# Two raw quads in the second MLP activation buffer, and a new order of operations searched with late transfers

## The chip, the cores and the metric

One core of a Trainium2 chip runs the whole program. The time is the device time of one execution in microseconds (us), given as the median of several executions.

PE is the matrix engine, PEld its weight loads, DVE the vector engine, ACT the scalar engine, POOL and SP two more engines that also issue transfers.

## The reference, cut to what matters

Random-feature attention on 8 batches of 8 heads, and then a mixer with a low-rank mix over the sequence and an MLP:

```python
proj = einsum('bhsd,md->bhsm', x, omega)             # for q and for k
phi  = concatenate([cos(proj), sin(proj)]) / sqrt(m)
kv   = einsum('bhsm,bhsd->bhmd', k_p, v);  z = sum(k_p)
num  = einsum('bhsm,bhmd->bhsd', q_p, kv); den = q_p . z
x    = num / den                                     # (8, 576, 512) after joining the heads
u    = x + (low-rank mix over the sequence with U, V)
out  = u + relu(u @ w_ch1) @ w_ch2                   # w_ch1: 512 x 2048
```

## The kernel before

The whole program is one list of words, ORDER, read from left to right. Each word emits one operation on one engine. Every engine runs its operations in that order, so **a word's place in the list is its place in the queue of its engine**; semaphores do the rest. `@n` names the first of the eight banks of PSUM (the memory that matmuls write) for the result; a bank is free again once another engine has copied it out.

```python
def run(self, order):
    for word in order.split():
        ...
        _, emit, needs, takes, frees = self.ops[name]
        if takes:
            self.banks[name] = range(int(at), int(at) + takes)   # PSUM banks, asserted free
        emit()
        for n in frees: ...                                      # banks free again
```

A *quad* is four heads: a q half and a k half (288 KB each as stored) and a v of 576 KB. A quad feeds two *groups* of two heads, and four groups make a batch: quads 0 and 1 feed groups 0 to 3, which are batch 0, while quads 2 and 3 belong to batch 1. The words that the argument needs:

```text
ld/k/2 ld/q/2  load the k or q half of raw quad 2 (POOL's queue)     ldv/1  load v of quad 1 (SP's queue)
tpp/q/2 tp/q/2 transpose that half on PE, copy it out on DVE         wv/1   widen v of quad 1 (POOL)
ak/5 uk/5      k angles of group 5: matmul on PE, "angle operation" on DVE (aq, uq the same for q)
s/4 c/4        sine, cosine of group 4 (ACT); p/4 the quarter turn between them (POOL)
kv/2 kvb/2     kv product of group 2 (PE), its copy out (DVE)        num/1  numerator of group 1 (PE)
x/3            normalised x of group 3 (DVE): the FOURTH x, batch 0 is then complete
w1/0/0         first complete W1 step of batch 0 (w1p: parts of it, ahead)    d  warmer: a dummy matmul
```

The raw buffers, two for q and k, and the load rule:

```python
rawp = ctx.enter_context(tc.tile_pool(name="rawp", bufs=2))
hidp = ctx.enter_context(tc.tile_pool(name="hidp", bufs=2))      # MLP activations, two buffers
...
def load(name, n):
    if ("raw", n) not in held:
        held["raw", n] = rawp.tile([P, 2, 2, NS * D], BF16, name="raw")
    return held["raw", n][:, "kq".index(name), :, :]
...
need = [r for r in read_raw(name, n - NRAW)] if n >= NRAW else []     # NRAW = 2: wait for the place
add(("ld", name, n), POOL, lambda ...: nc.gpsimd.dma_start(load(name, n), quad(src, n)), needs=need)
...
held["v", n] = rawp.tile([P, 2, NS * D], F32, name="vraw", bufs=2)
(nc.sync if n else nc.gpsimd).dma_start(held["v", n], quad(v, n))     # v of quad 0 by POOL, the rest by SP
```

The ORDER of the opening, cut, with banks and warmers left out:

```text
... ld/k/0 ... ld/q/0 ... ld/k/1 ... ld/q/1 ... ldv/0 omb ... ukh/0/0 ld/k/2 tp/q/0/0 ...
sq/0 tpp/q/1 ck/0 ldv/1 pq/0 tp/k/1 aq/1 tp/q/1 ld/q/2 cq/0 uq/1 ... W1/0 ldv/2 kv/0/0 ld/k/3 uq/2 ...
kvb/0 tpp/k/2 uq/3 tpp/q/2 c/1 p/2 num/0 ... x/0 ak/4 ld/q/3 wv/1 ... num/1 ... x/1 num/2 ... x/2 ... num/3 ... x/3 ...
tpp/k/3 ... tp/k/3 ... ak/5 ... uk/5 ... w1/0/0
```

Of the kernel before, what the change touches and what calls it, by code (L numbers as in the profile page):

```python
# [20 lines left out]
R = 32  # L21
# [14 lines left out]
begin first/k/0 first/k/1 ident first/q/0 om ld/k/0 d/0@5 warm d/1@1 ld/q/0 d/2@0 ld/k/1 d/3@7 d/4@5 ld/q/1 d/5@0 cast/k/1 cast/k/0 d/6@2  # L36
ldv/0 omb d/7@0 tpp/k/0/0@3 tpp/k/0/1@4 omt@7 tp/k/0/0 cast/q/0 WT tpp/k/0/2@0 tp/k/0/1 akh/0/0@5 tp/k/0/2 tpp/q/0/0@7 tpp/q/0/1@1 ukh/0/0
ld/k/2 tp/q/0/0 akh/0/1@2 tp/q/0/1 ukh/0/1 aq/0@4 d/8@6 gate skh/0/0 uq/0 d/9@7 low ak/1@0 skh/0/1 at/0@3 d/10@6 ut/0 pk/0 tpp/k/1@6 uk/1
sq/0 tpp/q/1@4 ck/0 ldv/1 pq/0 tp/k/1 d/11@1 aq/1@1 tp/q/1 ld/q/2 cq/0 uq/1 ak/2@3 wv/0 aq/2@6 uk/2 d/12@1 s/1 W1/0 ldv/2 kv/0/0@0 ld/k/3
uq/2 ak/3@2 W1/1 kv/0/1 p/1 uk/3 s/2 aq/3@6 kvb/0 tpp/k/2@2 uq/3 tpp/q/2@4 c/1 p/2 num/0 tp/k/2 tp/q/2 d/13@2 sk/3 x/0 ak/4@5 ld/q/3 wv/1  # L40
kv/1/0@3 c/2 uk/4 kv/1/1 pk/3 aq/4@1 kvb/1 kv/2/0@6 uq/4 sq/3 kv/2/1 lowc num/1 ck/3 kvb/2 kv/3/0@1 x/1 num/2 pq/3 kv/3/1 ld/k/4 hu0/0@0
cq/3 kvb/3 ut0x/0@3 huc0/0 hu0/1@4 ld/q/4 x/2 ut0/0 s/4 ut0x/1@0 W1/2 d/14@5 num/3 huc0/1 W1/3 ute0/0 hu0/2@7 ut0x/2@4 ut0/1 huc0/2
w1p/0/0@3 x/3 p/4 ut0/2 ute0/1 tpp/k/3@5 ute0/2 w1p/2/0@0 w1p/2/1 tp/k/3 hu0/3@7 w1p/1/0@2 w1p/3/0@1 huc0/3 ak/5@4 wv/2 c/4 w1p/3/1 uk/5
w1p/1/1 w1p/1/2 ut0x/3@7 ut0/3 w1p/3/2 w1p/2/2 w1p/0/1 ute0h/3 w1p/0/2 tpp/q/3@4 ute0/3 tp/4 w1/0/0 tp/q/3 aq/5@6 r/0/0 w1/0/1 w1/0/2 uq/5
w1/0/3 r/0/1 hn/0/0@4 r/0/2 w1/0/4@3 u/0/0 r/0/3 ldv/3 w1/0/5@0 r/0/4 s/5 ak/6@4 aq/6@1 w1/0/6@3 uk/6 w1/0/7@7 r/0/5 p/5 uq/6 r/0/6
w1/0/8@5 r/0/7 ak/7@0 r/0/8 aq/7@3 s/6 kv/4/0@6 uk/7 W2/0 w1/0/9@5 W2/1 kv/4/1 uq/7 W2/2 w1/0/10@2 r/0/9 p/6 c/5 hn/0/1@0 kvb/4 w1/0/11@5
u/0/1 num/4 wv/3 r/0/10 w1/0/12@4 x/4 r/0/11 w1/0/13@0 W2/3 r/0/12 d/15@1 kv/5/0@5 r/0/13 kv/5/1 s/7 ak/8@0 kvb/5 aq/8@3 w2/0/0/0@7 uk/8
num/5 c/6 p/7 uq/8 w1/0/14@0 w2/0/0/1 x/5 r/0/14 kv/6/0@1 ld/k/5 kv/6/1 c/7 ak/9@3 ld/q/5 w1/0/15@0 uk/9 ld/k/6 hnt/0@6 w2/0/0/2 ld/q/6
r/0/15 kvb/6 ut/tail/0 s/8 kv/7/0@3 kv/7/1 aq/9@5 num/6 kvb/7 num/7 x/6 p/8 w2/0/0/3 x/7 w2/0/1/0@0 w2/0/1/1 o/0/0 c/8 uq/9 w2/0/1/2 tp/5
hu/1@1 w2/0/1/3 s/9 huc/1 w2/0/2/0@7 o/0/1 hn/1/0@5 ldv/4 w2/0/2/1 p/9 st/0/0 u/1/0 hn/1/1@0 w2/0/2/2 u/1/1 w2/0/2/3 c/9 tu/1 w2/0/3/0@0  # L50
o/0/2 ak/10@2 ak/11@5 uk/10 w2/0/3/1 wv/4 tp/6 w2/0/3/2 uk/11 aq/10@3 w2/0/3/3 uq/10 kv/8/0@6 ldv/5 kv/8/1 kv/9/0@1 st/0/1 s/10 kvb/8
aq/11@4 kv/9/1 num/8 kvb/9 st/0/2 uq/11 w1/1/0@3 ldv/6 p/10 num/9 x/8 r/1/0 w1/1/1@4 s/11 o/0/3 w1/1/2@5 x/9 ld/k/7 w1/1/3@6 r/1/1 wv/5
w1/1/4@7 r/1/2 r/1/3 hnt/1@2 p/11 w1/1/5@0 r/1/4 ut/tail/1 c/10 ak/12@4 w1/1/6@1 uk/12 ld/q/7 w1/1/7@2 r/1/5 ld/k/8 r/1/6 ak/13@5 ld/q/8
r/1/7 kv/10/0@3 uk/13 aq/12@0 c/11 kv/10/1 w1/1/8@2 uq/12 w1/1/9@7 r/1/8 aq/13@5 kvb/10 tp/7 kv/11/0@0 r/1/9 uq/13 kv/11/1 s/12 num/10
w1/1/10@2 kvb/11 x/10 num/11 s/13 p/12 w1/1/11@5 x/11 tp/8 w1/1/12@3 w1/1/13@6 r/1/10 wv/6 r/1/11 hu/2@1 r/1/12 w1/1/14@0 r/1/13 huc/2
ld/k/9 c/12 w1/1/15@2 ld/q/9 hn/2/0@6 p/13 w2/1/0/0@3 u/2/0 r/1/14 hn/2/1@4 r/1/15 w2/1/0/1 u/2/1 c/13 ak/14@0 aq/14@6 w2/1/0/2 tu/2 uk/14
w2/1/0/3 uq/14 w2/1/1/0@0 o/1/0 kv/12/0@1 ldv/7 s/14 kv/12/1 ldv/8 kv/13/0@6 kvb/12 ak/15@3 st/0/3 kv/13/1 num/12 kvb/13 uk/15 tp/9 p/14
num/13 w2/1/1/1 x/12 w2/1/1/2 c/14 w2/1/1/3 x/13 wv/7 aq/15@1 ak/16@3 o/1/1 w1/2/0@6 uq/15 ld/k/10 w1/2/1@7 r/2/0 uk/16 ak/17@0 r/2/1
w1/2/2@6 s/15 uk/17 w1/2/3@5 w1/2/4@3 r/2/2 p/15 w1/2/5@2 r/2/3 r/2/4 hnt/2@0 w1/2/6@5 r/2/5 ut/tail/2 ld/q/10 aq/16@3 r/2/6 aq/17@6
kv/14/0@1 wv/8 c/15 kv/14/1 w1/2/7@5 kvb/14 uq/16 ld/k/11 num/14 w2/1/2/0@0 uq/17 s/16 w1/2/8@3 x/14 w2/1/2/1 tp/10 r/2/7 p/16 w1/2/9@4  # L60
r/2/8 kv/15/0@1 r/2/9 ak/18@5 st/1/0 kv/15/1 uk/18 aq/18@3 c/16 w2/1/2/2 ldv/9 w2/1/2/3 ldv/10 kvb/15 st/1/1 num/15 s/17 w1/2/10@7 x/15
w2/1/3/0@5 uq/18 r/2/10 w1/2/11@1 o/1/2 kv/16/0@6 r/2/11 ak/19@2 kv/16/1 s/18 st/1/2 wv/9 uk/19 aq/19@0 w2/1/3/1 ldv/11 w2/1/3/2 uq/19
wv/10 w1/2/12@4 kvb/16 ld/q/11 hu/3@2 r/2/12 ld/k/12 num/16 huc/3 w2/1/3/3 p/17 x/16 w1/2/13@1 hn/3/0@2 r/2/13 p/18 w2/2/0/0@7 u/3/0 c/17
w1/2/14@6 w1/2/15@0 r/2/14 hnt/3@1 hn/3/1@2 r/2/15 w2/2/0/1 s/19 u/3/1 w2/2/0/2 o/1/3 w2/2/0/3 ut/tail/3 c/18 st/1/3 p/19 w2/2/1/0@5 o/2/0
ak/20@0 st/2/0 kv/17/0@6 uk/20 w2/2/1/1 ld/q/12 c/19 tu/3 aq/20@3 kv/17/1 uq/20 ak/21@0 w2/2/1/2 kvb/17 w2/2/1/3 uk/21 tp/11 num/17
w2/2/2/0@4 x/17 s/20 w2/2/2/1 tp/12 o/2/1 kv/18/0@0 kv/18/1 aq/21@6 p/20 kv/19/0@2 kvb/18 kv/19/1 num/18 kvb/19 st/2/1 uq/21 w2/2/2/2
w2/2/2/3 x/18 s/21 num/19 ld/k/13 w1/3/0@0 x/19 w1/3/1@1 p/21 r/3/0 o/2/2 w1/3/2@7 r/3/1 ak/22@3 r/3/2 aq/22@1 ld/q/13 w1/3/3@0 uk/22 c/20
ld/k/14 w2/2/3/0@7 uq/22 w2/2/3/1 r/3/3 c/21 kv/20/0@5 ak/23@0 aq/23@3 kv/20/1 uk/23 w2/2/3/2 tp/13 s/22 w2/2/3/3 kvb/20 w1/3/4@0 o/2/3
uq/23 num/20 ldv/12 p/22 r/3/4 st/2/2 w1/3/5@7 hu/4@1 r/3/5 st/2/3 w1/3/6@3 huc/4 s/23 x/20 w1/3/7@2 w1/3/8@0 r/3/6 p/23 hnt/4@6 r/3/7
w1/3/9@5 ut/tail/4 r/3/8 w1/3/10@3 r/3/9 w1/3/11@0 wv/11 r/3/10 c/22 hn/4/0@6 ld/q/14 hn/4/1@2 u/4/0 w1/3/12@1 ld/k/15 ld/q/15 w1/3/13@4  # L70
u/4/1 r/3/11 wv/12 r/3/12 w1/3/14@7 r/3/13 tu/4 w1/3/15@6 r/3/14 ak/24@3 r/3/15 ak/25@0 uk/24 c/23 w2/3/0/0@7 tp/14 w2/3/0/1 uk/25
w2/3/0/2 kv/21/0@5 kv/21/1 aq/24@0 ak/26@2 kvb/21 w2/3/0/3 uq/24 num/21 o/3/0 w2/3/1/0@0 x/21 st/3/0 w2/3/1/1 uk/26 w2/3/1/2 w1/4/0@1
w1/4/1@5 r/4/0 aq/25@6 r/4/1 kv/22/0@1 uq/25 kv/23/0@3 s/24 kv/22/1 kv/23/1 w1/4/2@5 kvb/22 kvb/23 num/22 p/24 num/23 x/22 s/25 w2/3/1/3
x/23 w1/4/3@6 r/4/2 w1/4/4@7 p/25 o/3/1 r/4/3 hu/5@4 c/24 st/3/1 w2/3/2/0@2 huc/5 w2/3/2/1 r/4/4 aq/26@0 kv/24/0@3 kv/24/1 ak/27@5 kvb/24
w2/3/2/2 uq/26 w2/3/2/3 uk/27 w1/4/5@0 w1/4/6@1 o/3/2 r/4/5 num/24 r/4/6 w1/4/7@0 c/25 x/24 hn/5/0@1 hn/5/1@5 u/5/0 w1/4/8@4 r/4/7
w1/4/9@7 u/5/1 r/4/8 w2/3/3/0@0 r/4/9 tu/5 s/26 w2/3/3/1 aq/27@1 kv/25/0@3 uq/27 kv/25/1 ak/28@5 p/26 w2/3/3/2 st/3/2 kvb/25 s/27 uk/28
w1/4/10@2 ldv/13 w1/4/11@1 ldv/14 r/4/10 w1/4/12@7 p/27 r/4/11 num/25 r/4/12 w2/3/3/3 x/25 w1/4/13@2 o/3/3 w1/4/14@4 r/4/13 wv/13 c/26
w1/4/15@3 w2/4/0/0@7 ldv/15 st/3/3 w2/4/0/1 r/4/14 r/4/15 aq/28@5 tp/15 kv/26/0@0 uq/28 ak/29@2 kv/26/1 w2/4/0/2 uk/29 s/28 w2/4/0/3
w2/4/1/0@6 o/4/0 c/27 kvb/26 w1/5/0@2 p/28 st/4/0 w2/4/1/1 w1/5/1@7 r/5/0 c/28 hnt/5@3 w2/4/1/2 ut/tail/5 w2/4/1/3 r/5/1 w2/4/2/0@3 o/4/1
w1/5/2@2 num/26 r/5/2 w1/5/3@7 x/26 w2/4/2/1 r/5/3 w2/4/2/2 kv/27/0@0 ak/30@4 kv/27/1 uk/30 w2/4/2/3 w1/5/4@2 o/4/2 w1/5/5@5 kvb/27 r/5/4  # L80
w1/5/6@4 r/5/5 num/27 r/5/6 aq/29@2 x/27 ak/31@4 w2/4/3/0@7 uq/29 w2/4/3/1 w1/5/7@1 uk/31 w1/5/8@2 r/5/7 w1/5/9@5 r/5/8 s/29 w1/5/10@6
w1/5/11@1 w2/4/3/2 r/5/9 p/29 r/5/10 hu/6@0 r/5/11 w2/4/3/3 w1/5/12@2 o/4/3 wv/14 huc/6 w1/5/13@6 r/5/12 c/29 hn/6/0@0 hn/6/1@4 u/6/0
w1/5/14@7 w2/5/0/0@2 u/6/1 r/5/13 r/5/14 w1/5/15@0 tu/6 w2/5/0/1 r/5/15 kv/28/0@6 aq/30@4 aq/31@0 kv/28/1 w2/5/0/2 kvb/28 st/4/1 uq/30
w2/5/0/3 st/4/2 uq/31 w2/5/1/0@3 s/30 w2/5/1/1 st/4/3 w2/5/1/2 p/30 w2/5/1/3 num/28 w2/5/2/0@0 x/28 c/30 w2/5/2/1 o/5/0 w1/6/0@7 o/5/1
st/5/0 s/31 w2/5/2/2 st/5/1 w1/6/1@2 w1/6/2@5 r/6/0 p/31 r/6/1 w1/6/3@1 w1/6/4@2 wv/15 c/31 w2/5/2/3 w1/6/5@4 o/5/2 w1/6/6@3 st/5/2 r/6/2
# [57 lines left out]
def kernel(  # L143
# [125 lines left out]
    def load(name, n):  # L269
        if ("raw", n) not in held:  # L270
            held["raw", n] = rawp.tile([P, 2, 2, NS * D], BF16, name="raw")
        return held["raw", n][:, "kq".index(name), :, :]
# [427 lines left out]
```

## Time and profile before

| | kernel before |
|---|---|
| timed median | 358.21 us (358.04 to 358.26) |
| the execution that was profiled | 360.0 us, span 358.0 us |
| PE busy, share of the span | 341.3 us, 95% |
| raw q half of quad 2: issued, landed | 13.03, 21.94 us |
| v of quad 1: issued, landed | 11.69, 19.87 us |
| fourth x ends | 34.39 us |

The main lines are shown in the prediction. What the stop looks like on DVE is in the timeline of that engine (start, duration, operation, in brackets the idle time ahead and what ended it):

```profile
19.61 0.74 DVE L325 COPY T<-ps 128x1152 bf16<-128x1152 bf16 x1
23.16 0.76 DVE L325 COPY T<-ps 128x1152 bf16<-128x1152 bf16 x1 [2.81 <-PE ps L321]
24.27 0.23 DVE L458 RECIPROCAL ps<-ps 128x10 f32<-128x10 f32 x1 [0.34 <-PE ps L449]
```

DVE copies the k half of quad 2, has nothing for 2.81 us, and goes on with the q half once PE (L321) has transposed it.

I use two books for the opening. **The DVE book:** the fourth x ends at (end of DVE's second transposed copy, near 6 us) + (DVE's busy time from there) + (DVE's idle time from there). For this trace 5.60 + 23.67 + 5.12 = 34.39. **The PE book:** "lost" at a word is its start on PE minus the matrix work ahead of it in ORDER, counted at the full-clock spacing that the traces show, warmers left out. All kernels here do the same 331.6 us of such work ahead of the last half step, so what is lost there is what a kernel pays beyond it. At the last half step the book compares any two kernels well. At earlier words it is less exact where the work ahead differs (see the last part of the explanation).

### The profile page before, as it was taken

The page shows a single profiled execution, that of the slowest core. Times are in us where ns is not written, and L with a number is a line of the kernel's source. Part 1 is how long each engine was busy: PE and PEld are TensorE (multiplying, and loading weights), DVE is VectorE, ACT ScalarE, POOL GpSimd, SP SyncE. Part 2 cuts the span into 40 slices and gives each one's busy share as a digit, 9 for nine tenths or more (in the row PEclk, how much of TensorE's full clock was granted, in tenths as well). Part 3 has the DMA queues.
Part 4 walks back from the last instruction along what each step waited for, and adds up shares of the span by engine and source line. Part 5 has one row for each costly group of instructions (what it writes and reads, how often), then busy time and mean ns, then how long its engine had stood idle before and what let it go on. Part 6 is the DMA issues. An engine that isn't in the chain of part 4 may idle for free.

```text
span 358.0 us, 8213 instructions
## 1 busy us (share of the span) xinstructions
PE 341.3 (95%) x3544; PEld 180.4 (50%) x3585; DVE 193.2 (54%) x284; ACT 216.8 (61%) x223; POOL 117.3 (33%) x100
## 2 busy tenths in 40 slices
PE   7659999999999999989999999999999999999996
PEld 3446456454564554645455554554545544444444
DVE  3968868786687676866476754364320722000111
ACT  5868899559958877678829578437386004553210
POOL 5879185427634536324704043003230000000000
PEclk9869999999999999999999999999999999999999
DMA  8997989999999886999992086200722051511124
GB/s 173 224 239 116 203 142 195 217 178 227 192 194 192 123 246 128 115 177 166 196 183 46 3 212 140 62 3 0 148 60 44 2 104 29 117 31 29 37 53 88
DMA packets 68567, 45.06 MB, mean 126 GB/s; under 512 B 47156, under 2 KB 59828, under 8 KB 68532
## 3 DMA queue, kind: packets, MB, share of 16 engines
q1 hardware_dynamic: 55348, 30.09, 41.2%
q0 software_dynamic: 12816, 13.93, 25.5%
q8 instruction: 28, 0.46, 0.5%
q10 hardware_dynamic: 368, 0.52, 0.4%
q14 instruction: 7, 0.06, 0.1%
HBM read 37.16 MB, written 9.44 MB: 130 GB/s over the span
## 4 chain that ended last, share of the span: by engine, by line
PE 88%; DMA 7%; ACT 1%; issue 1%; POOL 1%; POOLq 0%
PE ps L610 35%; PE ps L630 34%; PE ps L430 5%; PE ps L444 4%; DMA raw<-in_q_dram 4%; DMA T<-raw 3%; PE ps L381 2%; PE ps L407 2%; PE ps L576 2%; PE ps L449 1%; PE ps L514 1%; ACT ft L416 1%; PE ps L321 1%; POOL ang L420 1%; PE ps L584 0%
## 5 line engine op out<-in xcount | busy, mean ns | idle before, releaser
L416 ACT ACTIVATE ft<-ang 128x2304 bf16<-128x2304 int16 (+2 forms) x67 | 134.1, 2020 | 35.4 <-DVE ang L359 15.3
L630 PE MATMUL ps<-W2b,hid 128*128 128x512 bf16 (+1 forms) x560 | 130.5, 373 | 2.6 <-issue 1.4
L623 ACT ACTIVATE hid<-ps 128x512 bf16<-128x512 f32 x144 | 81.9, 596 | 84.4 <-PE ps L610 83.9
L610 PE MATMUL ps<-uT,W1b 128*128 128x512 bf16 x512 | 121.7, 379 | 0.8 <-DMA uT<-u 0.6
L420 POOL TENSOR_SCALAR ang<-ang 128x2304 int32<-128x2304 int32 (+2 forms) x34 | 67.9, 2000 | 126.2 <-ACT ft L416 119.4
L359 DVE TENSOR_SCALAR ang<-ps 128x1280 int32<-128x1280 f32 (+2 forms) x66 | 84.8, 1313 | 24.7 <-PE ps L375 16.3
L630 PEld LDWEIGHTS <-hid 128*128 128x128 bf16 x592 | 55.4, 98 | 62.0 <-issue 2.1
L610 PEld LDWEIGHTS <-W1b 128*128 128x128 bf16 x576 | 54.3, 98 | 63.8 <-issue 1.4
L646 DVE TENSOR_TENSOR o<-ps,u 128x512 f32<-128x512 f32 x32 | 21.9, 686 | 52.1 <-PE ps L630 52.0
L430 PEld LDWEIGHTS <-ft 64*128 64x128 bf16 x1152 | 24.1, 96 | 9.9 <-issue 5.7
L430 PE MATMUL ps<-vq,ft 64*128 64x65 bf16 x1152 | 27.1, 193 | 1.4 <-DVE ang L359 0.9
L460 DVE TENSOR_TENSOR x<-ps,rec 128x640 bf16<-128x640 f32 x32 | 26.4, 825 | 1.1
L434 DVE CAST kvb<-ps 128x260 bf16<-128x260 f32 x32 | 13.4, 423 | 20.6 <-PE ps L430 19.8
L578 DVE TENSOR_TENSOR u<-ps,x 128x1024 bf16<-128x1024 f32 x16 | 19.2, 1221 | 9.6 <-PE ps L610 4.9
L305 POOL CAST vq<-vraw 128x1152 bf16<-128x1152 f32 x16 | 18.5, 1153 | 12.1 <-DMA vraw<-in_v_dram 12.1
L444 PEld LDWEIGHTS <-ft 128*128 128x128 bf16 x512 | 19.9, 99 | 5.0 <-issue 0.5
L444 PE MATMUL ps<-kvb,ft 128*128 128x65 bf16 x512 | 21.9, 195 | 0.0
L610 PE MATMUL ps<-utailT,W1b 128*128 128x512 bf16 x64 | 15.1, 379 | 0.0
L458 DVE RECIPROCAL ps<-ps 128x10 f32<-128x10 f32 x32 | 7.2, 224 | 13.8 <-PE ps L449 13.3
L381 PE MATMUL ps<-WT,T 64*128 64x128 bf16 x256 | 13.5, 222 | 1.1 <-DMA T<-raw 0.6
L298 POOL DMA_DIRECT2D raw<-in_k_dram x15 | 10.9, 725 | 10.2 <-ACT hid L623 6.3
L407 PE MATMUL ps<-T,WT 64*128 64x512 bf16 x64 | 13.2, 387 | 0.0
(58 smaller groups left out, 150.7 us busy)
## 6 DMA issues: line engine op xcount, KB each, us to landing
out_dram<-o SPq DMA_DIRECT2D x70, 128.0 KB, 2.4
vraw<-in_v_dram SPq DMA_DIRECT2D x15, 576.0 KB, 5.7
raw<-in_k_dram POOLq DMA_DIRECT2D x15, 288.0 KB, 5.7
raw<-in_q_dram POOLq DMA_DIRECT2D x15, 288.0 KB, 6.0
W1b<-in_moe_w_ch_dram POOLq DMA_DIRECT2D x4, 512.0 KB, 9.9
W2b<-in_moe_w_ch_dram POOLq DMA_DIRECT2D x4, 512.0 KB, 8.9
vraw<-in_v_dram POOLq DMA_DIRECT2D x1, 576.0 KB, 7.5
ang<-in_q_dram ACTq DMA_DIRECT2D x1, 288.0 KB, 3.5
```

Of the source, the lines that this page charges most:

```text
L359: nc.vector.tensor_scalar(out=dst, in0=src, scalar1=TO_UNITS, scalar2=None, op0=ALU.mult)
L381: nc.tensor.matmul(pk[:, e, i * P:(i + 1) * P], kT[r, c, :], WT[r, :])
L407: nc.tensor.matmul(pq[:, e, :], WT[r, :], transposed("q", n)[r, c:c + 4, :])
L416: nc.scalar.activation(out=held["ft", g].rearrange("p f a c -> p f (a c)")[:, f, lo:hi], in_=low[:, lo:hi, 0], func=ACT.Sin, scale=TO_RAD)
L420: nc.gpsimd.tensor_scalar(out=ang, in0=ang, scalar1=TURN / 4.0, scalar2=1.0, op0=ALU.add, op1=ALU.mult)
L430: nc.tensor.matmul(kv_ps[:, hh, o], ft[r, f, 0, c:c + M], vq[n % NV][r, NS * (g % 2) + s, :], start=(s == 0), stop=(s == NS - 1))
L444: nc.tensor.matmul(nd[:, hh, t, :], ft[:, f, 1, c:c + P], kvb[:, hh, f, :], start=(f == 0), stop=(f == 1))
L460: nc.vector.tensor_tensor(out=x[:, :, hp * P:(hp + 1) * P].rearrange("p t (h d) -> p h t d", h=2), in0=nd[:, :, :, 0:D], in1=rec.unsqueeze ...
L610: nc.tensor.matmul(one(key), W1b[:, f // 4, ct, f % 4 * P:(f % 4 + 1) * P], uT[:, :, ct, :], start=(ct == 0), stop=(ct == NCT - 1))
L623: nc.scalar.activation(out=held["hid", b][:, f, :], in_=one(at_bank), func=ACT.Relu)
L630: nc.tensor.matmul(one(key)[:, 0:cs.stop - cs.start], held["hid", b][:, f, t * P:(t + 1) * P], W2b[:, f, cs], start=(f == 0), stop=(f == N ...
L646: nc.vector.tensor_tensor(out=held["o", b, t][:, cs], in0=one(key)[:, 0:cs.stop - cs.start], in1=u[:, t, cs], op=ALU.add)
```

## The change

Its intent: raw quads 0 and 1 go into a part of the second MLP activation buffer that is unused until the MLP of batch 1, so quads 2 and 3 need not wait for a place; and the whole ORDER was searched anew, with all transfers except the opening ones assumed late, W1's pieces included.

```diff
-    low_f = hidp.tile([P, NFT, SM], BF16, name="hid").rearrange("p f t -> p (f t)").bitcast(F32)
+    low_h = hidp.tile([P, NFT, SM], BF16, name="hid").rearrange("p f t -> p (f t)")
+    low_f = low_h.bitcast(F32)
+    early_raw = [low_h[:, 2 * (S + NS * R) + n * 4 * NS * D: ...].rearrange(...) for n in range(2)]   # cut
...
-            held["raw", n] = rawp.tile([P, 2, 2, NS * D], BF16, name="raw")
+            held["raw", n] = early_raw[n] if n < 2 else rawp.tile([P, 2, 2, NS * D], BF16, name="raw")
...
-                need = [r for r in read_raw(name, n - NRAW)] if n >= NRAW else []
+                need = [r for x in "kq" for r in read_raw(x, n - NRAW)] if n >= NRAW + 2 else []
...     # relu of batch 1, the first writer of that buffer, waits for the transposes of quads 0 and 1
-    add(("r", b, f), SCA, relu, needs=[("w1", b, f)] + (... else ["lowc"] if b == 1 else []), ...)
+    add(("r", b, f), SCA, relu, needs=[("w1", b, f)] + (... else ["lowc"] + [r for n in range(2) for x in "kq" for r in read_raw(x, n)] if b == 1 else []), ...)
```

The opening of the new ORDER, cut to the words of the argument:

```text
... ld/q/1 ... ld/k/2 ... ldv/0 ... ld/q/2 ... ld/k/3 ... ld/q/3 ... W1/0 ... W1/1 ... W1/2 ...
... tpp/q/1 ldv/1 pq/0 ... num/0 c/1 tpp/k/3 p/2 x/0 aq/3 tp/k/3 ... uq/3 ak/4 ... uk/4 lowc aq/4 kv/1/0 ...
uq/4 wv/1 ak/5 sq/3 kvb/1 pk/3 kv/2/0 uk/5 num/1 ... x/1 kv/3/0 ... num/2 ... num/3 x/2 ... x/3 ... s/4 aq/5 ... w1/0/0
```

## The prediction

> **What bounds the kernel now.** The page first, parts 1 and 2:
>
> ```profile
> PE 341.3 (95%) x3544; PEld 180.4 (50%) x3585; DVE 193.2 (54%) x284; ACT 216.8 (61%) x223; POOL 117.3 (33%) x100
> ...
> PE   7659999999999999989999999999999999999996
> ...
> PEclk9869999999999999999999999999999999999999
> ```
>
> PE is busy 341.3 of 358.0 us, and its idle time sits in the first three to four slices of 9 us, which are also the only ones with a lowered clock. So what can be won lies in the opening 30 us; after that only removing matrix work or a stray wait helps. Second view, the busy time by stretches of the opening:
>
> ```profile
> 10.00:15.00 5.00, 2.67 (x28) 1.30 (x29) 5.00 (x7) 4.10 (x4) 3.86 (x5) 0.98 0.96 199
> 15.00:20.00 5.00, 3.61 (x57) 2.70 (x56) 5.00 (x6) 4.32 (x3) 5.00 (x5) 0.50 1.13 251
> 20.00:25.00 5.00, 3.01 (x40) 2.55 (x42) 1.78 (x5) 2.12 (x2) 3.13 (x3) 0.50 1.21 219
> 25.00:30.00 5.00, 3.95 (x146) 3.31 (x144) 4.84 (x8) 4.94 (x5) 4.37 (x6) 0.99 0.77 131
> ```
>
> The columns after the length are PE, PEld, DVE, ACT, POOL, then clock, DMA share, GB/s. From 10 to 20 us DVE is busy 10.0 of 10.0: the opening is bound by DVE, which empties PSUM (angles, transposed quads), not by PE. From 20 to 25 us DVE falls to 1.78 of 5: something stops everybody. Third view, the chain that ended last in its first 60 us, and PE's list of waits, name it:
>
> ```profile
> 13.03 8.91 DMA raw<-in_q_dram
> 21.99 1.14 PE ps L321 x9
> 23.13 0.88 PE ps L444 x16
> ...
> PE ps L321 <- DMA raw<-in_q_dram: 3.6, 3, 2.6
> ```
>
> The q half of raw quad 2 is issued at 13.03 us and lands at 21.9. PE runs in order; the transpose of that half (L321) stands ahead of num of group 0 (L444), so num/0, the normalisation and the features of groups 3 and 4 wait for data that only groups 4 and 5 need (a quad feeds two groups). DVE's idle time there is 2.81 us in one piece. Why issued so late: the raw buffer had two places, so the load of quad 2 had to follow the transposes of quad 0, and on the POOL queue it stood behind two angle operations.
>
> After 30 us I found one more stop worth naming, in the PE timeline: 0.61 us before W1 of batch 3 (waiting for uT) and 0.57 us before group 22 (waiting for T), 1.2 us together, where two DMA transposes follow each other on the SP queue.
>
> **What the Trainium skill says.** (1) "TensorE: Matmul & The Clock Gate", Part 1, "What's actually happening": an activity window of about 3.4 us decides the clock; an idle PE falls to half, and about 3.4 us of sustained work restores it. The trace agrees: 0.50 from about 15 to 25 us, nine transposes taking 1.14 us at half clock against 0.67 at full, and recovery after the dense stretch from 22 us on. (2) "DMA: Bandwidth & Descriptors", "Issuing engines are not separate DMA queues": transfers from all queues share 16 engines, so issuing from another queue gains no bandwidth. The trace agrees: quad 2's q took 8.9 us beside the low-rank loads, v and W1, at a DMA share above 1, against 5.1 us for an early half quad. (3) Same page, "Anatomy of one DMA — SWDGE (gpsimd) path": a fit of 2.0 us plus bytes over 436 GB/s. For a 576 KB read that would be an estimate of 3.4 us; this trace has 5.4 us or more, since the loads queue, so I use the trace's spacing.
>
> **The change part by part.**
>
> *Buffers.* Quads 0 and 1 go into the unused part of the second hidden buffer, so quads 2 and 3 need no place freed; both halves are issued at once. No instruction is added or removed apart from order: 20 warmers before and after. The hidden buffer is first written by relu of batch 1, at about 78 us; the transposes of quads 0 and 1 are over by 12 us, so the new dependency costs nothing.
>
> *Loads.* POOL issues one load per 0.72 us. In the new order: k2 at about 4.1, v0 at 4.8, q2 at 5.6, k3 at 6.3, q3 at 7.0, then W1/0 to W1/2 from 7.7. In the old trace the first quads land at 8.7 (k1), 10.2 (q1), 11.6 (v0), i.e. one 576 KB read per 1.45 us. On that spacing (estimate): k2 11.6, v0 13.1, q2 14.5, k3 16, q3 17.4, W1/0 and W1/1 by 25 us when v1, v2 and the low-rank pieces share the engines. PE first needs q2 at about 16.6 us and W1/0 at about 33. So the 2.6 us wait of PE goes. v0 gets 1.5 us later; POOL's widening of it then ends at 14.7, which the second cosine half (needed at about 16.7) can bear.
>
> *The DVE chain,* walked in the new order with the old trace's start-to-start costs (angles 1.40 and 1.14, transposed quad half 0.70, kv copy 0.35, reciprocal to x 1.2 us). Up to the second angle piece of group 0 the two are alike (8.0 us). Then gate, uq/0, ut/0 to 10.5; k1 copy, uk/1 to 12.6; q1 copy, uq/1, uk/2 to 15.9; k2 copy, uq/2, q2 copy, kvb/0, uk/3 to 20.2. The old trace stands at the same amount of work at 20.3 (it has uq/3, but not the q2 copy) and then idles 2.8 us. From 20.2 the new order does x/0, k3 copy, uq/3, uk/4, uq/4, kvb/1, uk/5, x/1, kvb/2, kvb/3, two hu copies, x/2, x/3: 12.0 us, so x/3 ends at 32.2 instead of 34.3, with the k3 copy and uk/5 already done and one uT copy and one hu copy fewer. ACT and POOL keep up, with little to spare: ck/3 at about 28.7 against the need at 29.1, cq/3 at 30.3 just ahead of num/3.
>
> *What it is worth on PE.* The end is set by when PE becomes continuously busy and by how much real work it has done by then. Counting matrix work at full-clock cost: the old kernel reaches the first complete W1 step (w1/0/0) at 38.2 us with 19.1 us of real work done (warmers left out), 19.1 us lost. The new one, by the walk, at about 35.7 us with 18.3 us done, 17.4 us lost. Gain **1.8 us** (rounded from the walk).
>
> *Against it: the clock.* From 10 to 32 us the new PE has about 12 us of work in 22 us and only two warmers (after num/3), while the old order had four there. It will fall to half clock as before and may still be at half when the dense part begins at 32 us, where the old kernel had been warm since 25. A full 3.4 us window at half clock costs 1.7 us; I charge a third of it, **0.6 us**.
>
> *Later.* With transfers assumed late in the search, the two stops of 1.2 us at 155 to 159 us should mostly go. In PE work between issue and use, the T transposes of the new order have between 6 and 30 us, loads 18 to 58 us (before 14 to 58). But the uT transposes of batches 4, 5 and 6 now have 7.0 to 7.8 us (before 10 to 16), and they take 6.1 us median. I book a gain of **0.8 us** and, as a risk, a loss of 0.2. Warmers in the dense part: two before (after W1 starts), one now, 0.2 us gained.
>
> Sum: 358.2 - 1.8 + 0.6 - 0.8 + 0.2 - 0.2 = **356.2 us**, that is 0.6% faster.
>
> **The rivals.** (a) *Matrix work is the bound and nothing is won (358):* the removed wait was one of the opening only, and another takes its place: POOL (5.0 of 5 busy at 15 to 20 us) now has nine loads and three W1 issues ahead of its first angle operation; if an issue waits for its completion slot, the cosines of group 0 move. For it: POOL has no slack in the walk. Against: the first angle operation is not needed before 11.6 us and the issues end by 10.9. (b) *The clock stays at half until 35 us or beyond:* 358 to 359. For it: PE's sparse opening and the fewer warmers; against: half clock makes the same work fill the PE to over 90%, which itself restores the clock. (c) *The chain shortens fully,* clock warm at 32 us and all later waits gone: 358.2 - 2.4 - 1.4 = 354.4, and with some luck in the DVE chain 353. Against more than that: DVE has no idle time left in the walk, so the opening cannot shrink further, and PE work after it is unchanged. (d) *Congestion:* 2.3 MB of raw quads now come before v0 and the low-rank factors; if the low-rank pieces land after 25 us (before: 18.5), POOL stops at their cast and hu/0 slips. It would cost up to 2 us; the shared queue speaks for it, 5 us of slack against.
>
> **Range and chances.** (c) gives the low end, (b) and (d) the high: 353.2 to 358.8. Faster by over 2% needs 351.0, which asks for 7.2 us; the whole opening loses 19 us, of which the DVE chain pins all but about 3. Chance 0.03. Slower by over 2% needs a new wait of 7 us in a kernel searched for late transfers: 0.01. Within 2%: 0.96.
>
> **What would show it right or wrong.** In the changed kernel's PE waits, the raw q wait of 2.6 us is gone, and the chain of the opening shows no long DMA piece between 13 and 22 us. DVE is busy over 4.7 of 5 in each stretch from 10 to 30 us. The fourth x (L464) ends at 31.5 to 33 us, and the first W1 matmul starts near 33. The clock row shows 0.5 somewhere between 12 and 32 us; if at 32 to 36 it is still half, (b) is at work. At 150 to 160 us PE busy rises from 8.77 to above 9.7. Wrong if DVE shows gaps of over 1 us before 30 us (POOL, ACT or a load holds it), or if a new DMA wait of over 1 us stands in PE's waits after 40 us.

## The result, and the profile after

| | before | after |
|---|---|---|
| median, same session | 358.24 us (358.04 to 359.32, 4 runs) | 359.13 us (358.85 to 359.81, 4 runs) |
| ratio | | 1.0022, 95% interval 0.9997 to 1.0046 |
| the same again, second session | 358.40 us | 359.52 us; 1.0042 (1.0022 to 1.0061) |

The changed kernel is not faster but slower by 0.2 to 0.4% (the first session's interval still includes no change, the second's does not), and the time lies above the predicted range.

From the page of the changed kernel, parts 1 and 2:

```profile
PE 345.0 (97%) x3549; PEld 182.6 (51%) x3585; DVE 193.9 (54%) x284; ACT 216.4 (61%) x223; POOL 117.4 (33%) x100
...
PE   7779999999999999999999999999999999999997
...
PEclk9758999999999999999999999999999999999999
```

PE's first slices are fuller than before (777 against 765), yet nothing is won: busy is not progress. PEclk is lower in slices two to four than before (7, 5, 8 tenths against 8, 6, 9), and matmuls at half clock fill more time (the nine transposes in the prediction took 1.14 us against 0.67). The stretches of the opening (length, PE, PEld, DVE, ACT, POOL with counts, then clock, DMA share, GB/s):

```profile
10.00:15.00 5.00, 3.38 (x41) 2.44 (x37) 5.00 (x6) 3.30 (x4) 3.30 (x4) 0.76 1.15 280
15.00:20.00 5.00, 4.45 (x75) 3.45 (x74) 4.34 (x6) 5.00 (x4) 3.19 (x3) 0.50 1.17 237
20.00:25.00 5.00, 3.88 (x62) 2.78 (x61) 4.93 (x8) 4.79 (x3) 5.00 (x6) 0.50 1.17 243
25.00:30.00 5.00, 4.27 (x122) 3.83 (x116) 4.22 (x8) 2.75 (x4) 4.34 (x5) 0.53 1.23 218
```

The hole of 20 to 25 us is gone: DVE 4.93 of 5, before 1.78. The wait on the raw q half is gone from PE's list. But the chain of waits that ended last has a new long transfer in it (start, duration, what):

```profile
11.44 13.99 DMA vraw<-in_v_dram
25.48 1.16 POOL vq L309
26.69 0.68 PE ps L434 x18
27.37 0.99 PE ps L448 x16
...
33.47 0.59 ACT uT L557
34.05 2.02 ACT ft L420
36.08 0.76 ACT uT L557 x2
```

v of quad 1 now takes 13.99 us from issue to landing, and lands at 25.43 us instead of 19.87. It goes through POOL's widening into kv of group 2 (L434) and num of group 1 (L448). Further on, the sine of group 4 (2.02 us on ACT) stands between two copies of uT that the W1 steps of batch 0 need. DVE's timeline between the first x and the second:

```profile
21.05 0.82 DVE L464 TENSOR_TENSOR x<-ps,rec 128x640 bf16<-128x640 f32 x1
21.79 0.75 DVE L329 COPY T<-ps 128x1152 bf16<-128x1152 bf16 x1
22.45 3.74 DVE L363 TENSOR_SCALAR ang<-ps 128x1024 int32<-128x1024 f32 x3
26.11 0.42 DVE L438 CAST kvb<-ps 128x260 bf16<-128x260 f32 x1
26.45 1.48 DVE L363 TENSOR_SCALAR ang<-ps 128x1280 int32<-128x1280 f32 x1
28.62 0.23 DVE L462 RECIPROCAL ps<-ps 128x10 f32<-128x10 f32 x1 [0.69 <-PE ps L453]
28.89 0.17 DVE L463 TENSOR_SCALAR rec<-ps 128x10 f32<-128x10 f32 x1
29.09 0.82 DVE L464 TENSOR_TENSOR x<-ps,rec 128x640 bf16<-128x640 f32 x1
```

The first x ends at 21.87 us, 3.4 us earlier than in the second trace of the kernel before (25.28, below). That is the wait that the change was to remove. The second x ends at 29.91 us, against 29.85: **8.0 us between the two x, and the whole gain is gone.** In that stretch stand the copy of quad 3's k half (0.75 us), four angle operations, one of them (1.48 us) for group 5 of the next batch, and 0.69 us of idle time behind the late v.

### The profile page after: what moved, and what is told of

It is laid out like the page before. It is cut to its first block, busy times and chain, and to the rows that moved or that the text cites. A ratio compares the mean times of both kernels' runs of the same rounds, so it can differ in the third digit from the quotient of the medians.

```text
span 357.3 us, 8216 instructions
## 1 busy us (share of the span) xinstructions
PE 345.0 (97%) x3549; PEld 182.6 (51%) x3585; DVE 193.9 (54%) x284; ACT 216.4 (61%) x223; POOL 117.4 (33%) x100
## 4 chain that ended last, share of the span: by engine, by line
PE 91%; DMA 4%; DVE 1%; issue 1%; ACT 1%; SPq 1%; POOL 0%; POOLq 0%; DVEq 0%
PE ps L614 35%; PE ps L634 35%; PE ps L434 5%; PE ps L448 5%; DMA vraw<-in_v_dram 4%; PE ps L385 2%; PE ps L411 2%; PE ps L580 2%; PE ps L232 2%; PE ps L453 1%; PE ps L518 1%; DVE ang L363 1%; ACT ft L420 1%; DVE T L329 0%; ACT uT L557 0%
## 5 line engine op out<-in xcount | busy, mean ns | idle before, releaser
L614 PE MATMUL ps<-uT,W1b 128*128 128x512 bf16 x512 | 119.3, 379 | 0.2
L434 PEld LDWEIGHTS <-ft 64*128 64x128 bf16 x1152 | 22.3, 98 | 8.1 <-issue 4.2
L434 PE MATMUL ps<-vq,ft 64*128 64x65 bf16 x1152 | 24.8, 196 | 1.3 <-POOL vq L309 0.7
L448 PEld LDWEIGHTS <-ft 128*128 128x128 bf16 x512 | 20.2, 100 | 5.2 <-issue 0.7
L448 PE MATMUL ps<-kvb,ft 128*128 128x65 bf16 x512 | 22.0, 197 | 0.1
L385 PEld LDWEIGHTS <-T 64*128 64x128 bf16 x256 | 8.6, 98 | 9.0 <-issue 8.3
L590 DVE TENSOR_TENSOR utail<-ps,x 64x512 bf16<-64x512 f32 x8 | 5.5, 684 | 13.9 <-PE ps L588 8.3
## 6 DMA issues: line engine op xcount, KB each, us to landing
W1b<-in_moe_w_ch_dram POOLq DMA_DIRECT2D x4, 512.0 KB, 20.2
```

Source lines behind the costliest of these rows:

```text
L385: nc.tensor.matmul(pk[:, e, i * P:(i + 1) * P], kT[r, c, :], WT[r, :])
L434: nc.tensor.matmul(kv_ps[:, hh, o], ft[r, f, 0, c:c + M], vq[n % NV][r, NS * (g % 2) + s, :], start=(s == 0), stop=(s == NS - 1))
L448: nc.tensor.matmul(nd[:, hh, t, :], ft[:, f, 1, c:c + P], kvb[:, hh, f, :], start=(f == 0), stop=(f == 1))
L614: nc.tensor.matmul(one(key), W1b[:, f // 4, ct, f % 4 * P:(f % 4 + 1) * P], uT[:, :, ct, :], start=(ct == 0), stop=(ct == NCT - 1))
```

## The experiments

In each diff only words of ORDER that move are shown (`-` where it stood, `+` where it stands now); where PSUM banks had to be chosen anew that is said. "Lost" and the DVE book are as defined above.

**1. The changed kernel again** (e1_same), unchanged, in the session of experiments 2 to 4.

> The changed kernel once more, five rounds beside the kernel before on one chip. The profiled spans so far are 357.3 us (changed) and 358.0 us (before), but the quoted times are 359.13 and 358.24 us from different sessions. Theory (the change gains about 0.8 us, all of it in the two transpose stops at 155 to 159 us): ratio 0.996 to 0.999. Rival (it is truly slower): ratio 1.001 to 1.004.

Measured 359.52 us (359.37 to 360.19), ratio 1.0042 (1.0022 to 1.0061), fourth x at 33.98. So it is slower by a small but real amount. Its clock was at half for two stretches of 6.83 us, where the first trace had one of 17.07.

**2. A warm clock** (e2_warm). 30 more dummy matmuls in PE's idle places from 8 to 26 us of the changed kernel.

```diff
- aq/0 tpp/k/1 gate ... ak/4 ... sq/3
+ aq/0 d d tpp/k/1 gate ... ak/4 d d ... d d d sq/3      # 30 warmers in all, cut
```

> The changed kernel with 30 more dummy matmuls put into PE's gaps between 8 and 26 us, nothing else changed. Clock theory (the opening's gain was eaten because the clock stayed at half from 12.6 to 29.7 us): the half-clock stretch shrinks from 17 us to under 7 us, the fourth x ends at about 32.3 us instead of 33.7, the span falls by 1.0 to 1.5 us, ratio to the changed kernel about 0.997. Rival (DVE and the loads set the pace whatever the clock): clock better, fourth x unchanged, span within 0.3 us. If the dummies crowd out work, the span grows.

Measured 358.50 us (357.95 to 360.87), ratio 1.0018 (0.9993 to 1.0044); the clock is at full from 6.8 us on. The fourth x ends at 33.59 us (33.74 and 33.98 without), and lost at the end is 19.89 us (20.03 and 20.28). Half clock costs the changed kernel up to 1.0 us by the medians of one session, 0.1 to 0.4 by the traces; it does not set when the fourth x comes.

**3. W1's second and third piece issued later** (e3_w1late), so that they leave the transfer engines to others.

```diff
- gate W1/1 ... at/0 W1/2
+ tpp/k/3 p/2 W1/1 ... pk/3 W1/2
```

> The changed kernel with the second and third W1 load issued later (after the angle operations of groups 2 and 3, about 22 and 28 us instead of 9 and 11). Congestion theory (v of quad 1 landed at 25.4 us, 14 us after its issue, because W1 shares the engines, and that held the widening, kv of group 2 and num of group 1): v lands before 22 us, PE's wait on vq of 0.7 us goes, the fourth x is about 0.7 us earlier, span 0.3 to 0.7 us shorter. Rival: v lands earlier but PE work at half clock takes up the gap, span within 0.2 us; or the later W1 holds back W1 of batch 0 after 40 us and the span grows by 1 us or more.

Measured 360.18 us, ratio 1.0057 (1.0039 to 1.0076). v of quad 1 still lands at 25.28 us. So W1's later pieces are not what holds it.

**4. The old order, with quad 2's loads early and nothing else** (e5_early2). The new buffers, the ORDER of before, and both halves of quad 2 loaded right behind v of quad 0.

```diff
- ukh/0/0 ld/k/2 tp/q/0/0 ... aq/1 tp/q/1 ld/q/2 cq/0
+ ldv/0 ld/k/2 ld/q/2 omb ... ukh/0/0 tp/q/0/0 ... aq/1 tp/q/1 cq/0
```

> The buffers of the change with the old order, and only the q load of quad 2 moved ahead of POOL's first angle operations. If the late q load was what cost the old opening, PE's waits on the raw q load (3.6 us in all) shrink to about 1 us, num of group 0 starts near 20 us instead of 22.8, and the span falls by 1 to 2 us against before. If the opening is bound by DVE and clock anyway, num of group 0 is early but the first complete W1 step comes at the same 38 us and the span stays within 0.5 us of before.

Measured **355.82 us** (355.06 to 356.90), ratio 0.9933 (0.9912 to 0.9954). Its DVE timeline, for the same stretch as above:

```profile
21.13 0.82 DVE L463 TENSOR_TENSOR x<-ps,rec 128x640 bf16<-128x640 f32 x1
21.87 1.48 DVE L362 TENSOR_SCALAR ang<-ps 128x1280 int32<-128x1280 f32 x1
23.27 0.42 DVE L437 CAST kvb<-ps 128x260 bf16<-128x260 f32 x1
23.60 1.21 DVE L362 TENSOR_SCALAR ang<-ps 128x1024 int32<-128x1024 f32 x1
24.73 0.41 DVE L437 CAST kvb<-ps 128x260 bf16<-128x260 f32 x1
25.20 0.23 DVE L461 RECIPROCAL ps<-ps 128x10 f32<-128x10 f32 x1
25.46 0.17 DVE L462 TENSOR_SCALAR rec<-ps 128x10 f32<-128x10 f32 x1
25.66 0.82 DVE L463 TENSOR_TENSOR x<-ps,rec 128x640 bf16<-128x640 f32 x1
```

The first x ends at 21.95 us, 0.1 us after the changed kernel's, but the second ends at 26.49, 4.5 us behind it instead of 8.0, with two angle operations between instead of four and a copy. The fourth x ends at 30.87; lost at the first complete W1 step is 15.93, at the end 15.99. So the prediction's mechanism, remove the wait on quad 2's q half, is right and is worth some 3 us in the opening that stay to the end. The clock is not what makes the difference: in this run it is at full from 5.8 us on, but the equally fast base of experiment 13 has 6.83 us at half clock, as many as the kernel before in experiment 5. The changed kernel has that gain at its first x and gives it away.

**5. The kernel before, traced a second time** (b1_before).

> The kernel before, traced once more. Its first trace belonged to a run of 360.0 us, while its timed runs have a median of 358.2 to 358.4. Theory: that trace was a slow draw, with 1.2 us lost in the two transpose stops at 155 to 159 us; a second trace shows a span of 356 to 357 us without those stops. Rival: the stops are always there and the span is 358 us again.

Measured 358.36 us, span 356.3: this is a typical execution, unlike the first trace. Its fourth x ends at 34.11, lost 19.04 at the first complete W1 step and 19.09 at the end, and it has the same stop on the raw q half (2.8 us in PE's waits). The stretch that the prediction booked 0.8 us for, in the first trace of the kernel before and then in the second:

```profile
150.00:160.00 10.00, 8.77 (x150) 5.28 (x151) 6.00 (x12) 5.81 (x6) 2.95 (x3) 1.00 1.31 168
150.00:160.00 10.00, 9.89 (x150) 5.65 (x144) 7.43 (x12) 6.59 (x8) 5.38 (x4) 1.00 1.14 168
```

PE is busy 9.89 of 10 in the second, 8.77 in the first. The two stops of 1.2 us belonged to that one execution of 360.0 us, not to the median of 358.2 from which the prediction took them.

**6. Quad 3 early, in the old order** (e8_early23). As experiment 4, with both halves of quad 3 loaded right behind quad 2, as the change does.

```diff
- ldv/0 ld/k/2 ld/q/2 omb ... kv/0/0 ld/k/3 uq/2 ... ak/4 ld/q/3 wv/1
+ ldv/0 ld/k/2 ld/q/2 ld/k/3 ld/q/3 omb ... kv/0/0 uq/2 ... ak/4 wv/1
```

> The old order with the new buffers and both raw quads 2 and 3 issued ahead of everything else, as the change does, so the same load order as the change except for W1 (e5 had only quad 2's q half moved). If the new load order is harmful by itself (v of quad 1 and the low-rank pieces pushed back), the time goes from e5's 355.8 back towards 358. If it is the order of the compute work alone, it stays within 0.5 us of 355.8.

Measured 359.35 us, ratio 1.0029 (1.0011 to 1.0048): **loading quad 3 early costs all that the early quad 2 had won.** v of quad 1 is issued at 11.12 us and lands at 24.52, so POOL's widening of it stands idle, and PE's first line of waits is:

```profile
24.58 1.14 POOL L308 CAST vq<-vraw 128x1152 bf16<-128x1152 f32 x1 [4.06 <-DMA vraw<-in_v_dram]
...
PE ps L433 <- POOL vq L308: 3.4, 1, 3.4
```

The queues say why. From the transfers between 9 and 20 us (packets, MB, share of the 16 engines; q0 is POOL's queue, q1 the one with SP's loads), the second trace of the kernel before:

```profile
q1 hardware_dynamic: 839, 1.44, 53.3%
q0 software_dynamic: 768, 1.19, 50.3%
```

and the changed kernel:

```profile
q0 software_dynamic: 1311, 1.84, 81.0%
q1 hardware_dynamic: 559, 0.93, 35.3%
```

The total grows little, from 2.63 to 2.77 MB. What quad 3 and W1 gained on POOL's queue, v and the low-rank factors lost on SP's. Experiments 4 and 6, which differ in quad 3's loads alone, show the same in this window: POOL's queue goes from 1.33 to 1.78 MB, SP's from 1.43 to 1.01. The Trainium skill, "DMA: Bandwidth & Descriptors", section "Queues, rings and completion order", says that each transfer engine goes round the queues packet by packet; the trace agrees that both queues advance together, but the shares follow the load, not a fixed half. On SP's queue v also stands behind the low-rank pieces, the last of which lands at 22.56 us in the changed kernel and at 18.25 in the second trace of before.

**7. The kernel before with one word moved** (e9_oldbuf), no new buffers at all: the q half of quad 2 is issued at 8.70 us, ahead of POOL's two quarter turns of group 0.

```diff
- aq/1 tp/q/1 ld/q/2 cq/0
+ akh/0/1 tp/q/0/1 ld/q/2 ukh/0/1
```

> The kernel before with its own two raw buffers; only the q load of quad 2 moved ahead of POOL's two angle operations of group 0, to about 9 us instead of 13. If the place in POOL's queue was the trouble and not the number of buffers, the load lands at about 16 us and the time is within 0.5 us of e5's 355.8. If the buffers are needed, it stays above 357.

Measured 356.37 us (355.22 to 359.35), ratio 0.9947 (0.9915 to 0.9979); the half lands at 16.16 us, the fourth x ends at 31.31, lost 16.29 at the end. The time lies 0.55 us above experiment 4, between the two outcomes that were named. Most of the gain was to be had without the buffers: the place on POOL's queue held the load, not the room for it. Whether the rest of the difference to experiment 4 is real the intervals do not tell.

**8. The lateness of v undone in the old order** (e10_v1first). Experiment 6, with v of quad 1 moved to POOL's queue ahead of quad 3.

```diff
- (nc.sync if n else nc.gpsimd).dma_start(held["v", n], quad(v, n))
+ (nc.sync if n > 1 else nc.gpsimd).dma_start(held["v", n], quad(v, n))
- ldv/0 ld/k/2 ld/q/2 ld/k/3 ld/q/3 ... ck/0 ldv/1 pq/0
+ ldv/0 ld/k/2 ld/q/2 ldv/1 ld/k/3 ld/q/3 ... ck/0 pq/0
```

> e8 (old order, new buffers, quads 2 and 3 loaded first, 359.4 us) with one transfer moved: v of quad 1 goes out on POOL's queue ahead of quad 3. Theory (what hurts is that loads nobody needs before 34 us push v of quad 1, needed at 21 us, to 24.5 us): v lands before 19 us, PE's wait of 3.4 us on its widened copy goes, num of group 1 returns from 26.9 to about 24.4 us, the time to 355.5 to 356.5. Rival (the sheer amount of loading hurts other transfers too, as the low-rank pieces): stays above 357.5.

Measured 356.82 us (355.51 to 357.88), ratio 0.9954 (0.9930 to 0.9978). v lands at 16.99 us, and PE no longer waits on it. Quad 3 is early here too, so in the old order it did its harm by way of v: 356.27 with quad 3 late as well (experiment 11, same session) lies within the intervals. The time is 0.3 us above the expected range. The profiled execution (357.42 us) was a slow draw from the start: PE waited 1.7 us for a k half of quad 0 that landed at 7.14 us (5.46 to 6.38 in the two traces of before), so num of group 1 came at 26.70 instead of the 24.4 expected and the fourth x at 33.09.

**9 and 10. The same in the changed kernel** (e11_v1first_new, e12_v1wv_new): first the load of v alone, then also its widening on POOL moved ahead.

```diff
- tpp/q/1 ldv/1 pq/0                  # first
+ ld/q/2 ldv/1
- uq/4 wv/1 ak/5                      # second, on top of the first
+ ck/0 p/1 wv/1 tpp/q/2
```

> The changed kernel with v of quad 1 moved ahead of quad 3 on POOL's queue, its order of work untouched. v lands before 19 us instead of 25.4; POOL's widening keeps its late place behind the low-rank casts. If lateness of v alone costs the changed kernel its gain, the time falls by 1.5 us or more to under 358. If the order was built around late transfers and cannot use the early one, the time stays within 0.7 us of the changed kernel's 359.5.

> As e11, and the widening of v of quad 1 moved ahead of the angle operation of group 2 on POOL. If the late place of the widening was the one remaining cause, the fourth x comes at about 33 us and the time falls another 0.5 us. If the order of the other work (angle of group 5 and the quad 3 copy ahead of the fourth x, late kv of groups 1 and 2) holds it, no change against e11.

Measured 360.00 us (1.0044, 1.0025 to 1.0062) and 360.32 us (1.0058, 1.0040 to 1.0075). v lands at 17.97 and 17.60 us, and the wait on it is gone in both, yet the fourth x ends at 35.20 and 34.88, where experiment 10 expected about 33. Neither gains: **the late v is a sufficient cause in the old order, but undoing it does not repair the new one.**

The two runs are not a clean test, though. One more load stands on POOL's queue, and the third W1 issue waits for a load there (0.72 and 0.68 us), so POOL's first quarter turn, which started at 11.68 us in the changed kernel, comes at 12.29 and 12.84, ACT waits 2.02 and 2.48 us for it instead of 1.38, and the first x ends at 22.50 and 23.05 instead of 21.87. That is the prediction's rival (a), brought in by the repair. It does not hide a large gain: from the start of the first x's reciprocal to the end of the fourth x, experiment 10 takes 13.11 us and the changed kernel 13.15, while experiment 4 takes 10.20. That the new order is arranged around late arrivals is a reading, not shown.

**11. The good order with v early as well** (e13_best), and q of quad 3 late.

```diff
- ukh/0/0 ld/k/2 ... ck/0 ldv/1 pq/0 ... tp/q/1 ld/q/2 cq/0 ... ak/4 ld/q/3 wv/1
+ ldv/0 ld/k/2 ld/q/2 ldv/1 omb ... num/2 pq/3 ld/q/3
```

> An attempt to beat both kernels: new buffers, old order of work, q of quad 2 and v of quad 1 early on POOL's queue, q of quad 3 issued after POOL's angle operations of group 3. Against e5 (355.8 us) POOL is relieved of one load and one wait before cos of group 3, so the fourth x should come about 0.5 us earlier than 30.9: 355.0 to 355.8 us. If v early costs the opening loads, it is no better than e5.

Measured 356.27 us (355.33 to 358.58), ratio 0.9951 (0.9922 to 0.9979), lost 16.03: no better than experiment 4. With v at 21.6 us nothing had waited for it.

**12. The new order without the work put ahead.** The changed kernel, with the copy of quad 3's k half and group 5's angles moved behind the fourth x (e6_x3first); banks chosen anew from num/0 on.

```diff
- c/1 tpp/k/3 p/2 x/0 aq/3 tp/k/3 ... wv/1 ak/5 ... kv/2/0 uk/5 num/1 ... s/4 aq/5 huc0/2 ... huc0/3 uq/5
+ ut0/3 tpp/k/3 ... w1p/1/1 tp/k/3 ... w1p/0/2 ak/5 uk/5 ... w1p/2/1 aq/5 u/0/0 uq/5
```

> The changed kernel with its own loads and its own later order; only the work that the new order put ahead of the fourth x on DVE (copy of the k half of quad 3, 0.7 us; angle of group 5, 1.4 us, with their matmuls) is moved behind it. DVE-order theory (the new order spends the won time on work that nobody waits for yet): the fourth x ends 1.5 to 2.1 us earlier than 33.9, at about 32, and the time falls by 1 to 2 us against the changed kernel. Rival (the loads or POOL hold the opening): fourth x within 0.5 us of 33.9, time within 0.5 us.

Measured 363.90 us, ratio 1.0146 (1.0127 to 1.0166), a miss. With the filling gone, the late v lay bare: PE waits 2.5 us on its widening, and DVE idles 2.35 us ahead of the second x. Two causes mixed, so the next three runs were made to take them apart.

**13 and 14. The work put ahead, added to the good order** (e17_base, e15_ahead). The base is the old order with quad 2's q half, v of quad 1 and quad 3's k half early; the second run adds to it only the trait in question, at about the places that the new order gives it (banks chosen anew from num/0 on).

```diff
- ut0/2 ute0/1 tpp/k/3 ... w1p/2/1 tp/k/3 ... huc0/3 ak/5 ... w1p/3/1 uk/5        # second against base
+ c/2 uk/4 tpp/k/3 ... kvb/1 tp/k/3 ... uq/4 ak/5 ... kvb/2 uk/5 kv/3/0 x/1
```

> Old order, new buffers; q of quad 2 and v of quad 1 early on POOL's queue, k of quad 3 behind them, q of quad 3 late. The reference for the next run. Expected as e5 and e13: 356.0 to 356.5, fourth x (L463/L464) ends near 31.0, no wait of PE on a raw load or on vq over 0.5 us before 32 us.

> e17_base plus one trait of the new order: the copy of quad 3's k half and the angle operation of group 5 stand ahead of the fourth x on DVE (banks of PSUM chosen anew between num/0 and the first W1 steps). Theory 'work put ahead on DVE costs its own time': 0.7 + 1.4 = 2.1 us more DVE work ahead, fourth x ends 1.5 to 2.1 us later (32.5 to 33.1), and since the same work is later missing behind it, PE gets part back: time 0.5 to 1.8 us over e17_base. Rival 'it is free, the new order loses elsewhere (late kv, ACT copies, clock)': fourth x as in e17_base and time within 0.4 us.

Measured: base **355.79 us** (354.57 to 359.07), ratio 0.9924 (0.9883 to 0.9964); with the work ahead **360.39 us** (358.39 to 361.63), ratio 1.0034 (1.0001 to 1.0067). The second's DVE timeline between first x and second:

```profile
24.22 0.75 DVE L328 COPY T<-ps 128x1152 bf16<-128x1152 bf16 x1
24.88 1.21 DVE L362 TENSOR_SCALAR ang<-ps 128x1024 int32<-128x1024 f32 x1
26.97 0.43 DVE L437 CAST kvb<-ps 128x260 bf16<-128x260 f32 x1 [0.87 <-PE ps L433]
27.31 1.48 DVE L362 TENSOR_SCALAR ang<-ps 128x1280 int32<-128x1280 f32 x1
28.71 0.22 DVE L461 RECIPROCAL ps<-ps 128x10 f32<-128x10 f32 x1
```

The copy (24.22) and group 5's angle (27.31) are the only added work. In the DVE book the base is 5.52 + 23.64 + 2.41 = 31.57 us and the second 5.42 + 25.70 + 3.38 = 34.50: 2.06 us of work, and 0.97 us of idle time besides. Part of that idle time is due to the banks chosen anew: kv of group 2 takes a bank of quad 3's k half and waits 0.63 us on PE until DVE has copied it, so this share need not come with the work. PE loses 2.84 us by it (19.40 against 16.56 at the end), and the two profiled executions differ by 2.83 us (358.39 and 355.56). The medians differ by more, 4.6 us; the profiled execution of the second was its fastest of six, and no trace shows the others. Both exceed what was expected (fourth x 1.5 to 2.1 us later, time 0.5 to 1.8 us). The rival "it is free" has fallen. The base is, with experiment 4, the best version: both beat the two kernels compared, by 0.7 to 0.8% against before.

**15. And taken away from the new order with v in time** (e16_x3first_v): experiment 10 with the moves of experiment 12.

> The changed kernel with v of quad 1 early and widened early (as e12) and with the copy of quad 3's k half and the angle operation of group 5 moved behind the fourth x (as e6). If the work put ahead was what kept e12 back: fourth x 1.5 to 2 us earlier than e12's 34.9, time 358.3 to 359.2. If the order of kv and num or the ACT copies hold it: fourth x stays at 34 to 35 and the time at 360 or above, as in e6 a new wait shows (name it from the waits of DVE and PE).

Measured 363.97 us, ratio 1.0136 (1.0110 to 1.0161). In the DVE book, experiment 10 is 5.90 + 25.37 + 3.61 = 34.88 us and this one 6.46 + 23.23 + 4.54 = 34.23 (34.22 in the trace): of 2.14 us of work removed, 0.93 come back as idle time and 0.56 as a later start of the opening. And group 5's angles, now just ahead of W1, block it there; from its ACT timeline:

```profile
43.74 2.12 ACT L419 ACTIVATE ft<-ang 128x2304 bf16<-128x2304 int16 x1 [3.50 <-DVE ang L362]
45.77 2.53 ACT L626 ACTIVATE hid<-ps 128x512 bf16<-128x512 f32 x5
```

ACT waits 3.50 us for an angle, then five relus come at once, and PE loses 21.27 us by the first complete W1 step but 24.54 eight steps later. So this run does not show what the new order would do with that work well placed. It does show something left over: with v in time and the work moved away, DVE still idles 2.44 us between the first x and the fourth (0.60 in experiment 4), 1.35 us of it ahead of the second x, waiting for num of group 1. **Left open:** how the rest of the new order's loss splits between the late kv and num of groups 1 and 2, the banks, and the work put ahead. No run takes the new order's late words apart one by one.

## Why the prediction was wrong

*The wait on quad 2's q half goes:* right. It is absent from PE's waits, the first x comes 3.4 us earlier, and experiments 4 and 7 show it worth 2.6 and 2.4 us of the median (358.40 - 355.82, and 358.73 for before in that session - 356.37).

*"-1.8 for the opening" is the first term that failed.* Its step was the DVE walk: "DVE has no idle time left in the walk", with x/3 at 32.2. The fourth x came at 33.74. Laid beside the trace, the walk is 0.4 us early from the start (the second angle piece of group 0 ends at 8.44 us, not 8.0), is right up to the first x (it starts at 20.59, not 20.2), and then gives 12.0 us to the fourth x where 13.15 passed. **That difference is idle time: DVE stands for 1.15 us there**, 0.69 of it ahead of the second x, behind the late v. The work itself was counted rightly, the copy of quad 3 and the angle of group 5 included.

Against the kernel before, in the DVE book: the changed kernel is 6.46 + 25.19 + 2.09 us, the typical kernel before 5.95 + 23.68 + 4.48, experiment 4 5.96 + 23.54 + 1.37. The change took 2.4 us of idle time away and put 1.5 us of work and 0.5 us of later start in its place. The walk booked the extra work as done "already", a gain; experiments 13 and 14 show that ahead of the fourth x such work is paid for in full. By the PE book the opening gained at most 19.04 - 18.67 = 0.4 us, not 1.8 (the prediction's own figures give 19.1 - 17.4 = 1.7).

*Rival (d), congestion, named the right thing and watched the wrong transfer.* It gave the low-rank pieces 5 us of slack (and put all four raw quads, 2.3 MB, ahead of v of quad 0, where in the new ORDER only quads 0 and 1 and the k half of quad 2 precede it). They landed 4.3 us later, and v of quad 1 behind them 5.9 us later than in the second trace of before (25.43 against 19.53), with none to spare. The prediction took the widening of v of quad 0 into account and not that of quad 1, which the transfers it moved forward also share engines with. Experiments 6 and 8 show it as cause in the old order; in the new order it costs 0.7 us of PE's waits, since the work put ahead fills the time.

*Rival (a), POOL's queue:* POOL's second and third W1 issue did wait, 0.75 and 0.66 us, until loads of quad 1 had landed, but its first quarter turn at 11.68 us waited for ACT after that, not for the issues. It is not the cause in the changed kernel; in experiments 9 and 10, with one load more on that queue, it does cost time.

*"+0.6 for the clock":* 17.07 us at half clock in the first trace where a third of a 3.4 us window was booked. The length was off, but the cost was small all the same: 0.1 to 1.0 us by experiment 2. Rival (b) is not the cause. Its counter-argument, that a busier PE would bring the clock back by itself, did not hold: PE was busy 4.45 of 5 us from 15 to 20 us and the clock stayed at half until 29.67.

*"-0.8 for the transpose stops":* it failed, because it was subtracted from a median that never had them (experiment 5). That PE is busy 9.79 of 10 us there now, as foretold, says nothing. The page showed it beforehand: the profiled run took 360.0 us and the median was 358.2.

*A loss that no term had:* at the last half step the changed kernel has lost 20.03 us and the kernel before 19.09, so it is 0.9 us worse there, although it was no worse at the first complete W1 step. By the book the opening gained 0.4 us and 1.3 were lost behind it (20.03 - 18.67, less 19.09 - 19.04). The split is uncertain: it hangs on what a q angle is charged, whose two matmuls overlap (0.22 to 0.42 us from its start to the next word's), and with that range a recount gives the opening 0 to 0.2 us and what follows about 1. PE's waits from 36 to 60 us account for 0.3 us of it, a wait for the copy of quad 3's q half. The rest is open. The sine of group 4 between the uT copies, which the chain shows, is not it as far as PE tells: PE is busy 2.99 of the 3.00 us from 34 to 37.

The sum 358.36 + 0.9 = 359.3 lies near the measured 359.13, but that is no independent check, since both spans went into it. The terms of 0.2 for warmer and uT slack were too small to see. Of the stated tests, the DVE stretches (4.34 and 4.22 where 4.7 was asked), the fourth x, the first W1 matmul (34.39 us, not 33), and the absence of a long transfer in the chain all came out against the prediction; no new DMA wait over 1 us stands after 40 us, as foretold. One of its readings compares unlike things: the load of 5.1 us set against quad 2's 8.9 us is half as large.

## What to carry to other kernels

When a wait is removed, ask of every transfer moved forward which other transfer then lands later, and of every operation moved forward whether the step that opens the main phase needs it: here work for the next batch was not free on the engine that bounds this one (2.06 us in experiment 14). Try the smallest edit that removes the wait first; here moving one quad's loads won 0.5 to 0.7% where the new order with new buffers lost 0.2 to 0.4%. And before a stop in a trace is subtracted from a median, compare the profiled run's own time with that median.

## What the Trainium skill lacked or had wrong

- "DMA: Bandwidth & Descriptors", "Queues, rings and completion order", states packet-wise rounds between queues, but not what share a queue then gets. Here the bytes on the queue with SP's loads fell from 1.44 to 0.93 MB in 11 us when the POOL queue was given more to do (1.19 to 1.84 MB), and one 576 KB load went from 7.9 to 14.0 us.
- The same page, "Anatomy of one DMA — SWDGE (gpsimd) path": its fit gives 3.4 us for 576 KB (estimate by that page). Loads of this size on POOL's queue took 7.4 us in the second trace of before and 10.8 in experiment 8; the fit has no term for other transfers in flight, and so does not serve a shared opening.
- "TensorE: Matmul & The Clock Gate", "What's actually happening", calls the window free-running and the ramp variable between runs, and advises not to fit it. The runs agree and add the size: stretches at half clock were multiples of 3.41 us (6.83, 10.24, 17.07), and one and the same kernel had 17.07 us in one run and 13.66 in another; keeping the clock up gained at most 1.0 of 359.5 us.
- No page that I drew on says that a profiled execution can be a slow draw: 360.0 us against a median of 358.2, with 1.2 us of stops that a second trace did not have.
